# Attention and MLP mixer on one core: the first batch element's last bank sums, one scaling step and the weight conversions are placed anew

## Chip, core and metric

The kernel runs on one core of a Trainium2 chip. The metric is the device time of one execution in microseconds (us), as the median of several runs. The core has five engines with an instruction queue each: TensorE (PE in the profile; its weight loads are listed as PEld), VectorE (DVE), ScalarE (ACT), GpSimd (POOL) and SyncE (SP), which here only issues DMAs.

## What is computed

For each of 8 batch elements: attention of 12 heads with normalized q and k (448 positions, 64 dimensions a head), then an MLP mixer on the 448 x 768 result.

```python
def rmsnorm(x, g):
    return x / np.sqrt(np.mean(x * x, axis=-1, keepdims=True) + 1e-06) * g
q_n, k_n = rmsnorm(q, g_q), rmsnorm(k, g_k)
scores = (1 / np.sqrt(64)) * np.matmul(q_n, k_n.transpose(0, 1, 3, 2))
attn = softmax(scores)                      # over the last axis
attn_out = np.matmul(attn, v)               # (8, 12, 448, 64)
x = attn_out.transpose(0, 2, 1, 3).reshape(8, 448, 768)
h = np.maximum(x.transpose(0, 2, 1) @ w_tok1, 0.0) @ w_tok2     # 256 wide inside
u = x + h.transpose(0, 2, 1)
out = u + np.maximum(u @ w_ch1, 0.0) @ w_ch2                    # 1536 wide inside
```

q, k, v and the two g are float32. The four weight matrices of the mixer come in as float64; [...] the kernel reads them as pairs of 32-bit words and puts float32 numbers together from them.

## The kernel before

**Order of the work.** The heads are handled in 48 pairs, six pairs to a batch element. While the mixer of element b runs, the attention of element b+1 is worked in between, so that TensorE always has something to do. The order on TensorE, VectorE, ScalarE and GpSimd is the order in which the program issues the instructions; it is fixed by lists of items, each a cost and a function, which `merge` interleaves in proportion to their costs. Only the order on SyncE's queue is left to the scheduler.

**Attention.** `att_step(g)` is one of four steps s = 0 to 3 for two pairs of heads (t counts these groups, n is the first of the two pairs that come next). A step has scores on TensorE (L381), exponentials on ScalarE (L385), the products with v (L454), and sums of exponentials on VectorE (L422). Beside these it prepares the next two pairs: squares (L1269, L1272, ScalarE), their sums over the head (L1286, VectorE), a fold (L1294, ScalarE), a first guess of the inverse root (L1303, L1308, VectorE), Newton steps (on GpSimd, L1316 to L1319, for pairs 1 to 11 and from 20 on; else on VectorE, L1327 to L1329), the scaling of q and k by it (L343, VectorE, one instruction for each pair), and the turning of q and k so that the head dimension lies on partitions. Pairs 0 to 11 are called plain: TensorE turns them (L355) and ScalarE copies them out with g (L361, L363). Later pairs are turned by VectorE (L358) and then scaled by ScalarE (L361). In `att_step` the functions listed in `behind` go to the end of a step and those in `turns` next to its scores.

**Mixer.** The token part is two products: tok1 (L755, with the Relu by ScalarE, L758) and tok2 (L763), whose result VectorE adds from PSUM into the tile uT (L768). `m_tile()` gives out the PSUM banks of the mixer; a new product has to wait until the bank that it gets was read. The channel part of elements 1 to 7 uses a Strassen-like scheme of seven products (ch1 L879, ch2 L936) with weight units that SyncE loads (L810) from a scratch tensor in DRAM. Its right-hand sides are partly sums of quarters of uT, made by `moving_sums`: T1 and T2 by VectorE (L784, L785), T3 and T4 by GpSimd (L786, L787).

**Element 0.** Its channel part uses plain products, `first_stage(n)`, 36 stages n: 0 to 17 for w_ch1, 18 to 35 for w_ch2, six terms t to an output tile, two PSUM banks at a time (L851). After the last term of a w_ch1 tile ScalarE writes the Relu out (L863). After the last term of a w_ch2 tile ScalarE copies each of the two banks into an SBUF tile r (L860), and GpSimd adds that into uT (L861). When an output tile is done, VectorE turns it (`trans_y`, L972) and SyncE sends it (L699).

**Weight conversion.** It happens during attention and mixer of element 0, in 40 chunks, one step of the chain to a slot. Slot i does, in this order: the last step of chunk i-3 (`convert_last`, L302, VectorE), the loads of chunk i+2 (L176, SyncE), the first step of chunk i (`convert_first`: L268, L269, L271, L273, VectorE), the second step of chunk i-2 (L279, ScalarE), and the store of a finished chunk into the scratch tensor (L192, SyncE). Four chunks are token weights; the other 36 feed the 36 stages. The first 14 slots (`BEFORE`) lie in the attention of element 0, six in the token part of its mixer, and the other 24, k = 0 to 23, behind the products: slot k is placed behind product `begins(k)` in `first_items`. From the converted chunks GpSimd also makes the sums of weights that the seven products need (`make`, L204 to L207), which go to the scratch tensor (L211); to make some of them, stored chunks are read back (L221, L240).

Of the kernel before, what the change touches and what calls it, by code (L numbers as in the profile page):

```python
# [13 lines left out]
ALU = mybir.AluOpType  # L14
# [12 lines left out]
def merge(*lists):  # L27

    totals = [sum(c for c, _ in l) or 1.0 for l in lists]
    done = [0.0] * len(lists)  # L30
    at = [0] * len(lists)
    res = []
    while True:
        live = [i for i in range(len(lists)) if at[i] < len(lists[i])]
        if not live:
            return res
        i = min(live, key=lambda i: (done[i] + lists[i][at[i]][0] / 2) / totals[i])
        c, fn = lists[i][at[i]]
        at[i] += 1
        done[i] += c  # L40
        res.append((c, fn))
# [3 lines left out]
def whole(ctx, tc, shifted, pre, q, k, v, g_q, g_k, moe_w_tok1, moe_w_tok2, moe_w_ch1, moe_w_ch2, out):  # L45


    nc = tc.nc
# [61 lines left out]
    st = dict(pre.st)  # L110
# [43 lines left out]
    def columns(i):  # L154
        src = chunks[i][1][0]
        return WCOLS if chunks[i][2] is None or len(src.shape) == 3 else src.shape[-1]

    def raw_tile():
        return raw_pool.tile([P, WCOLS, 2], U32, name="raw")

    def weight_load(i):
        rows, srcs, dst = chunks[i]
        wide = srcs[0].dtype == I64
        t = raw_tile()
        flat = t[0:rows].rearrange("p n w -> p (n w)")
        if not wide:
            t = t[:].rearrange("p n w -> p (n w)").bitcast(F32)
            flat = t[0:rows]
        n = columns(i) // len(srcs) * (1 + wide)
        for k, src in enumerate(srcs):  # L170
            to = flat[:, k * n:(k + 1) * n]
            if wide:
                src = src.bitcast(U32)
            if len(src.shape) == 3:
                to = to.rearrange("p (i n) -> p i n", i=src.shape[1])
            nc.sync.dma_start(out=to, in_=src)  # L176
        st["raw", i] = t
# [12 lines left out]
    def store(j):  # L190

        nc.sync.dma_start(out=slots(j, 0, 4), in_=st["stage", j])  # L192
# [63 lines left out]
    def wide(i):  # L256
        return 0 <= i < len(chunks) and chunks[i][1][0].dtype == I64

    def words(i):

        return [st["raw", i][0:chunks[i][0], 0:columns(i), w] for w in range(2)]

    def convert_first(i):

        if wide(i):
            lo, hi = words(i)
            m = cv_sb[0:chunks[i][0], i % 2, 0:columns(i)].bitcast(U32)
            nc.vector.tensor_scalar(m, hi, 0x000FFFFF, 0x00100000, ALU.bitwise_and, ALU.bitwise_or)  # L268
            nc.vector.scalar_tensor_tensor(  # L269
                out=lo.bitcast(F32), in0=lo, scalar=2.0**-32, in1=m, op0=ALU.mult, op1=ALU.add)  # L270
            nc.vector.scalar_tensor_tensor(  # L271
                out=lo, in0=hi, scalar=0x80000000, in1=lo, op0=ALU.bitwise_and, op1=ALU.bitwise_or)
            nc.vector.tensor_scalar(hi, hi, 0x7FF00000, None, ALU.bitwise_and)  # L273

    def convert_second(i):

        if wide(i):
            e = words(i)[1]
            nc.scalar.activation(out=e, in_=e, func=AF.Relu, bias=expo_c[0:chunks[i][0], 0:1], scale=8.0)  # L279
# [14 lines left out]
    def convert_last(i):  # L294
        rows, srcs, dst = chunks[i]
        n = columns(i)
        if dst is None:
            dst = stage_home(i - len(first))
            st["stage", i - len(first)] = dst.rearrange("p (q n) -> p q n", q=4)
        if wide(i):  # L300
            lo, hi = (w.bitcast(F32) for w in words(i))
            nc.vector.scalar_tensor_tensor(  # L302
                out=dst, in0=lo, scalar=2.0**-20, in1=hi, op0=ALU.mult, op1=ALU.mult)
        else:
            nc.gpsimd.tensor_copy(out=dst, in_=st["raw", i][0:rows, 0:n])
        st.pop(("raw", i))

    def weight_items(lo, hi):

        def one(i):  # L310
            if 0 <= i - 3 < len(chunks):
                convert_last(i - 3)
            if 3 <= i and i + 2 < len(chunks):
                weight_load(i + 2)
            convert_first(i)
            convert_second(i - 2)
            if 0 <= i - 4 - len(first):
                store(i - 4 - len(first))
        return [(1.0, lambda i=i: one(i)) for i in range(lo, hi)]

# [16 lines left out]
    def scale(p):  # L339

        x, d = pre.by_rows(p, st["qk", p])
        r = st.pop(("rs", p))
        nc.vector.tensor_tensor(out=x, in0=x, in1=r.unsqueeze(2).to_broadcast(list(x.shape)), op=ALU.mult)  # L343
# [235 lines left out]
    def att_step(g):  # L579


        t, s = divmod(g, 4)
# [3 lines left out]
        items = []  # L586
# [46 lines left out]
        n = p + 2  # L633
        ahead, behind, turns = [], [], []
        f = lambda fn, *pairs: [lambda i=i: fn(i, st) for i in pairs]
        scales = lambda n: [lambda i=i: scale(i) for i in (n, n + 1)]
        if g in (1, 5):
            ahead, behind = f(pre.square, g // 4 * 2 + 4), f(pre.reduce, g // 4 * 2 + 4)
        elif g in (2, 6):
            ahead, behind = f(pre.square, g // 4 * 2 + 5), f(pre.reduce, g // 4 * 2 + 5)  # L640
        elif g in (3, 7):
            behind = pre.roots(g // 4 * 2 + 4, st)
        elif g in (4, 8):
            behind = scales(g // 4 * 2 + 2)
        if live and n < NP:
            late = n < 2 * NPAIR + 2
            if t >= NPAIR // 2 and late:
                if s == 1:
                    ahead, behind = f(pre.square, n), f(pre.reduce, n) + f(pre.square, n + 1)
                elif s == 2:  # L650
                    behind = f(pre.reduce, n + 1) + pre.roots(n, st) + scales(n)
            elif t >= NPAIR // 2:
                a, b = f(pre.square, n) + f(pre.reduce, n), f(pre.square, n + 1) + f(pre.reduce, n + 1)
                behind = (a, b + pre.roots(n, st), scales(n), [])[s]
            now = {2: [] if pre.plain(n) else [n], 3: [n, n + 1] if pre.plain(n) else [n + 1]}.get(s, [])
            turns = [lambda q=q, i=i: turn_qk(q, i) for q in now for i in (1, 0)]
# [165 lines left out]
    def r_tile(i):  # L822
        return r_pool.tile([P, 2 * HS], F32, name=f"r{i}")
# [16 lines left out]
    def first_stage(n):  # L840

        w, _, m, t = stages[n]
        wide = w is moe_w_ch2
        last = (KF if wide else KC) - 1
        if t == 0:
            st["m", 0], st["m", 1] = m_tile(), m_tile()
        a, u = st.pop(("stage", n)), st["uT", 0]
        for o in range(2):
            ps = st["m", o][:, 0:S]
            for half in range(2):  # L850
                nc.tensor.matmul(  # L851
                    out=ps, lhsT=a[:, o + 2 * half, :],
                    rhs=natural(half)[:, :, t, :] if wide else u[:, half * KC + t, :],
                    start=(t == 0 and half == 0), stop=(t == last and half == 1))
            if t < last:
                continue
            if wide:

                to, c = u[:, o * KC + m, :], r_tile(1 + o)[:]
                nc.scalar.copy(out=c, in_=ps)  # L860
                nc.gpsimd.tensor_tensor(out=to, in0=to, in1=c, op=ALU.add)  # L861
            else:
                nc.scalar.activation(  # L863
                    out=natural(o)[:, :, m, :], in_=ps.rearrange("p (i n) -> p i n", i=2), func=AF.Relu)
        st["used"].add(("stage", n))
# [150 lines left out]
    def first_items(tok, prods, some):  # L1016


        convert = weight_items(BEFORE, len(chunks) + 4)
        items = merge(tok, convert[:6])  # L1020
        for j, it in enumerate(prods[:-6]):
            items.append(it)
            items += [(0.0, convert[6 + k][1]) for k in range(len(convert) - 6) if begins(k) == j]
            if j % 2 and j < 2 * len(some):
                items.append(some[j // 2])
            if j in (26, 28):

                items += turns(0, [y_order(0)[j // 2 - 13]])
        return items, prods[-6:]

    def begins(k):


        return 2 + -(-k * 14 // 10) if k < 10 else min(k + 9, 29)

    def last_items(b):

# [6 lines left out]
    stages = stage_list()  # L1044
# [20 lines left out]
    for p in (4, 5):  # L1065
# [7 lines left out]
        out=g_t[:, 0:1], in0=g_t[:, 0:1], scalar=float(D) ** 0.5, in1=g_t[:, 1:2],  # L1073
# [27 lines left out]
    for b in range(B):  # L1101
# [4 lines left out]
        else:  # L1106
# [5 lines left out]
            begin, early = merge(tok1_items(b, 1) + early[:3 * KC], left[2:]), early[3 * KC:]  # L1112
            if b == 1 and not shifted:
                run(merge(begin, sums[5:9]))
                early, double = merge(early, sums[9:20]), merge(double, sums[20:])
                begin = []
            elif b == 1:
                early, double = merge(begin + early, sums[5:20]), merge(double, sums[20:])
                begin = []
            early = begin + early + double  # L1120
            early, last = early[:-4], early[-4:]
        lo = (b + AHEAD) * per + 1
# [281 lines left out]
```

## Time and profile before

| what | value |
|---|---|
| runs, us | 1308.59, 1310.11, 1312.26; median 1310.11 |
| the profiled execution: own time | 1311.39 us |
| its span, first to last instruction | 1309.6 us |
| granted TensorE clock, mean | 0.994 |
| idle of PE before element 0's first turns (L355), at the start | 15.2 us |
| idle of DVE in 195 to 199 us | 3.73 of 4.00 us |
| idle of DVE in 205 to 225 us | 0.72 of 20.00 us |
| idle of DVE in 256 to 275 us | 16.01 of 19.00 us |
| idle of PE in 420 to 1300 us | 1.12 of 880.00 us |

The span is what the timeline covers; the execution's own time is 1.8 us longer. The profile's times are counted from the first instruction. "idle before <- releaser" in a group's row is the time for which the engine stood still just before these instructions, and what ended it. Busy times by engine don't add up to the span, as the engines work side by side. Lines of the timeline give the start, the duration, the engine, the line of the program, the operation and the tiles; x3 at the end means that three equal instructions were put together, and the duration is then from the first start to the last end.

### The profile page before, as it was taken

What the parts mean: (1) busy time and instruction counts of PE and PEld (TensorE: products, weight loads), DVE (VectorE), ACT (ScalarE), POOL (GpSimd) and SP (SyncE); (2) the same over time, 40 slices, a digit from 0 to 9 for tenths busy, and PEclk for the clock granted to TensorE, in tenths of its full rate; (3) what the DMA queues carried; (4) which work ended last, traced back from release to release, by engine and by line L of the source; (5) the groups of instructions that cost most, each with busy time, mean ns of one, the idle gap of its engine ahead of it and who ended that gap; (6) DMA issues with size and microseconds to landing.
All of it is one profiled execution on the core that took longest, in us unless ns stands there. A gap on an engine that the chain in (4) does not pass through costs nothing.

```text
span 1309.6 us, 20269 instructions
## 1 busy us (share of the span) xinstructions
PE 1264.2 (97%) x7408; PEld 930.7 (71%) x7408; DVE 763.4 (58%) x1205; ACT 373.5 (29%) x740; POOL 350.6 (27%) x575
## 2 busy tenths in 40 slices
PE   5998999989998999999999999999999999999996
PEld 3444444447777688796778777796788868797996
DVE  6998768827774466645765366654666266433212
ACT  5652423213331133302441044302332033200100
POOL 1302410447352122221332122321242123111220
PEclk9999999999999999999999999999999999999999
DMA  9667485899979676686649667694757864385554
GB/s 207 171 190 179 122 218 149 196 257 254 246 203 225 146 186 157 156 224 121 163 122 233 141 152 175 157 235 98 169 151 174 204 139 142 117 224 132 172 177 83
DMA packets 502450, 228.07 MB, mean 174 GB/s; under 512 B 374532, under 2 KB 464004, under 8 KB 502340
## 3 DMA queue, kind: packets, MB, share of 16 engines
q1 hardware_dynamic: 489218, 224.83, 68.9%
q10 hardware_dynamic: 12994, 1.84, 0.8%
q8 instruction: 61, 1.00, 0.3%
q14 instruction: 49, 0.40, 0.1%
q0 software_dynamic: 128, 0.00, 0.0%
HBM read 187.07 MB, written 39.52 MB: 173 GB/s over the span
## 4 chain that ended last, share of the span: by engine, by line
PE 79%; DVE 9%; DMA 4%; SPq 3%; issue 2%; ACT 1%; POOL 1%; DVEq 0%; ACTq 0%; POOLq 0%
PE m_ps L936 25%; PE m_ps L879 25%; PE s_ps L381 8%; PE o_ps L454 8%; PE m_ps L763 5%; PE m_ps L755 5%; PE m_ps L851 3%; DVE raw L269 1%; DVE raw L271 1%; PE d_ps L434 1%; DMA qk_t<-in_k_dram 1%; DMA raw<-in_moe_w_ch_dram 1%; DVE stage L302 1%; DVE ms L1286 1%; DMA hb<-in_q_dram 1%
## 5 line engine op out<-in xcount | busy, mean ns | idle before, releaser
L936 PE MATMUL m_ps<-hb,unit 128*128 128x224 f32 x1764 | 339.8, 353 | 4.1 <-DVE uT L945 2.4
L936 PEld LDWEIGHTS m_ps<-hb,unit 128*128 128x128 f32 x1764 | 332.2, 190 | 15.2 <-issue 12.5
L879 PE MATMUL m_ps<-tu,unit 128*128 128x224 f32 x1008 | 201.9, 355 | 0.1
L879 PEld LDWEIGHTS m_ps<-tu,unit 128*128 128x128 f32 x1008 | 189.0, 190 | 14.6 <-issue 9.9
L385 ACT ACTIVATE e<-s_ps 128x448 f32<-128x448 f32 x294 | 138.3, 551 | 205.6 <-PE s_ps L381 197.5
L879 PE MATMUL m_ps<-uT,unit 128*128 128x224 f32 x756 | 151.1, 354 | 0.0
L879 PEld LDWEIGHTS m_ps<-uT,unit 128*128 128x128 f32 x756 | 142.2, 190 | 7.0 <-issue 4.6
L381 PE MATMUL s_ps<-qkT 64*64 64x448 f32 x1260 | 142.2, 545 | 0.4 <-ACT x L735 0.4
L454 PE MATMUL o_ps<-e,v 64*64 64x448 f32 x1148 | 129.1, 538 | 0.2
L422 DVE TENSOR_TENSOR es<-es,e 128x896 f32<-128x896 f32 x90 | 109.7, 1219 | 14.1 <-ACT e L385 8.9
L945 POOL TENSOR_TENSOR uT<-uT,r 128x448 f32<-128x448 f32 (+1 forms) x56 | 56.6, 1020 | 228.3 <-DVE r L945 140.9
L884 DVE TENSOR_TENSOR r<-m_ps,r 128x448 f32<-128x448 f32 x63 | 39.2, 622 | 108.1 <-PE m_ps L879 55.7
L945 DVE TENSOR_TENSOR uT<-uT,m_ps 128x448 f32<-128x448 f32 (+1 forms) x70 | 33.8, 499 | 110.9 <-PE m_ps L936 110.9
L381 PEld LDWEIGHTS s_ps<-qkT 64*64 64x64 f32 x1260 | 44.8, 132 | 67.1 <-issue 59.2
L454 PEld LDWEIGHTS o_ps<-e,v 64*64 64x64 f32 x1148 | 45.2, 133 | 62.4 <-issue 58.0
L884 POOL TENSOR_TENSOR hb<-r,r 128x448 f32<-128x448 f32 x21 | 24.0, 1145 | 235.6 <-ACT r L900 235.6
L763 PE MATMUL m_ps<-w_sb,h 128*128 128x448 f32 x192 | 78.3, 561 | 8.9 <-DVE uT L768 8.9
L755 PE MATMUL m_ps<-x,w_sb 112*128 112x384 f32 x256 | 84.5, 487 | 1.0 <-ACT x L735 1.0
L755 PEld LDWEIGHTS m_ps<-x,w_sb 112*128 112x128 f32 x256 | 48.4, 190 | 34.3 <-ACT x L735 1.3
L763 PEld LDWEIGHTS m_ps<-w_sb,h 128*128 128x128 f32 x192 | 36.5, 195 | 46.8 <-issue 27.8
L885 ACT ACTIVATE hb<-hb 128x448 f32<-128x448 f32 x63 | 36.3, 577 | 116.7 <-DVE hb L884 98.1
L1286 DVE TENSOR_REDUCE ms<-sq 128x28 f32<-128x896 f32 (+2 forms) x44 | 47.5, 1079 | 35.2 <-ACT sq L1272 32.2
(122 smaller groups left out, 1372.8 us busy)
## 6 DMA issues: line engine op xcount, KB each, us to landing
unit<-ws SPq DMA_DIRECT2D x294, 384.0 KB, 4.1
raw<-in_moe_w_ch_dram SPq DMA_DIRECT2D x72, 256.0 KB, 3.6
v<-in_v_dram SPq DMA_DIRECT2D x96, 112.0 KB, 3.7
xs<-xt SPq DMA_DIRECT2D x56, 168.0 KB, 4.7
x<-xs SPq DMA_DIRECT2D x14, 672.0 KB, 6.9
out_dram<-turned SPq DMA_DIRECT2D x168, 56.0 KB, 2.0
qk_t<-in_q_dram SPq DMA_DIRECT2D x144, 56.0 KB, 3.3
qk_t<-in_k_dram SPq DMA_DIRECT2D x144, 56.0 KB, 3.9
```

Of the source, the lines that this page charges most:

```text
L381: nc.tensor.matmul(out=pss[i][rows_of(i, a), 0:S], lhsT=qkT[h, 1, k * D:(k + 1) * D], rhs=qkT[h, 0, :], start=True, stop=True)
L385: nc.scalar.activation(out=e[:, i, :], in_=pss[i][:, 0:S], func=AF.Exp)
L422: nc.vector.tensor_tensor(out=es[:], in0=(es if k > 1 else st["e", t, 0])[:], in1=st["e", t, k][:], op=ALU.add)
L454: nc.tensor.matmul(out=st["o", p][a * D:(a + 1) * D, 0:S], lhsT=vt[rows, k * D:(k + 1) * D], rhs=e[rows, :], **kw)
L755: nc.tensor.matmul(out=ps[:, 0:HC], lhsT=w1_sb[0:R, c, jc * P:(jc + 1) * P], rhs=st["x", b, h][0:R, :, c, :], start=(c == 0), stop=(c == N ...
L763: nc.tensor.matmul(out=ps[:, 0:S], lhsT=st["h1", jc][:, cc * P:(cc + 1) * P], rhs=w2_sb[:, jc].rearrange("p c r -> p (c r)"), start=(jc == ...
L851: nc.tensor.matmul(out=ps, lhsT=a[:, o + 2 * half, :], rhs=natural(half)[:, :, t, :] if wide else u[:, half * KC + t, :], start=(t == 0 an ...
L879: nc.tensor.matmul(out=ps[:, j * HS:(j + 1) * HS], lhsT=w[:, t, j, :], rhs=m, start=(t == 0), stop=(t == KC - 1))
L884: add = lambda e, o, x, y: e.tensor_tensor(out=o, in0=x, in1=y, op=ALU.add)
L936: nc.tensor.matmul(out=ps[:, j * HS:(j + 1) * HS], lhsT=st["w"](j, t), rhs=hb[:, HB[what], t, :], start=(t == 0), stop=(t == KF - 1))
L945: add = lambda e, o, x, y: e.tensor_tensor(out=o, in0=x, in1=y, op=ALU.add)
L1286: self.nc.vector.tensor_reduce(out=st["ms", p][:, p % 2, lo:hi], in_=sq[:, lo:hi], axis=AX_X, op=ALU.add)
```

## The change

There are four parts.

1. Slots of the conversion are three items instead of one. `convert_first` is split into `mantissa` (L268, L269) and the rest (L271, L273). The items are: the last step with the loads; `mantissa`; the rest, the second step and the store. Each has a cost of 0.3 instead of 1.0 for the whole. `first_items` is adapted to the threefold list.
2. In `att_step` the scaling (`scales(n)`) of two plain pairs from t = 3 on moves from the end of step s = 2 to the end of step s = 3. This concerns pairs 8, 9 and pairs 10, 11.
3. In the last stage, n = 35, VectorE adds both banks from PSUM into uT, in place of ScalarE's copy and GpSimd's add.
4. `begins(k)`: from k = 10 on, slots are placed two products earlier.

```diff
-    def convert_first(i):
+    def mantissa(i):
         if wide(i):
             lo, hi = words(i)
...
             nc.vector.scalar_tensor_tensor(
                 out=lo.bitcast(F32), in0=lo, scalar=2.0**-32, in1=m, op0=ALU.mult, op1=ALU.add)
+
+    def convert_first(i):
+
+        if wide(i):
+            lo, hi = words(i)
             nc.vector.scalar_tensor_tensor(
                 out=lo, in0=hi, scalar=0x80000000, in1=lo, op0=ALU.bitwise_and, op1=ALU.bitwise_or)
             nc.vector.tensor_scalar(hi, hi, 0x7FF00000, None, ALU.bitwise_and)
...
     def weight_items(lo, hi):

-        def one(i):
+        def end(i):
             if 0 <= i - 3 < len(chunks):
                 convert_last(i - 3)
             if 3 <= i and i + 2 < len(chunks):
                 weight_load(i + 2)
+
+        def begin(i):
             convert_first(i)
             convert_second(i - 2)
             if 0 <= i - 4 - len(first):
                 store(i - 4 - len(first))
-        return [(1.0, lambda i=i: one(i)) for i in range(lo, hi)]
+        parts = (end, lambda i: mantissa(i), begin)
+        return [(0.3, lambda i=i, fn=fn: fn(i)) for i in range(lo, hi) for fn in parts]
...
                 elif s == 2:
-                    behind = f(pre.reduce, n + 1) + pre.roots(n, st) + scales(n)
+                    behind = f(pre.reduce, n + 1) + pre.roots(n, st) + scales(n) * (not pre.plain(n))
+                elif s == 3 and pre.plain(n):
+                    behind = scales(n)
...
             if wide:
                 to, c = u[:, o * KC + m, :], r_tile(1 + o)[:]
+                if n == len(stages) - 1:
+                    nc.vector.tensor_tensor(out=to, in0=to, in1=ps, op=ALU.add)
+                    continue
                 nc.scalar.copy(out=c, in_=ps)
                 nc.gpsimd.tensor_tensor(out=to, in0=to, in1=c, op=ALU.add)
...
-        items = merge(tok, convert[:6])
+        items = merge(tok, convert[:18])
         for j, it in enumerate(prods[:-6]):
             items.append(it)
-            items += [(0.0, convert[6 + k][1]) for k in range(len(convert) - 6) if begins(k) == j]
+            items += [(0.0, fn) for k in range(len(convert) // 3 - 6) if begins(k) == j
+                      for _, fn in convert[18 + 3 * k:21 + 3 * k]]
...
-        return 2 + -(-k * 14 // 10) if k < 10 else min(k + 9, 29)
+        return 2 + -(-k * 14 // 10) if k < 10 else min(k + 7, 29)
```

## The prediction

> **What bounds the kernel now.** I read the busy times first, then TensorE's waits, then the timeline round each wait, then busy times by stretch.
>
> ```profile
> PE 1264.2 (97%) x7408; PEld 930.7 (71%) x7408; DVE 763.4 (58%) x1205; ACT 373.5 (29%) x740; POOL 350.6 (27%) x575
> ```
>
> TensorE is the bound: 1264.2 of 1309.6 us. The change removes no matmul, so all it can win lies in the 45 us in which TensorE stands still, plus matmuls that run at half clock after a stop. Its waits:
>
> ```profile
> PE t_ps L355 <- DVE g_t L1072: 15.2, 1, 15.2
> PE m_ps L763 <- DVE uT L768: 8.9, 3, 4.8
> PE m_ps L851 <- ACT r L860: 2.8, 1, 2.8
> PE m_ps L936 <- DVE uT L945: 2.4, 1, 2.4
> PE m_ps L851 <- DVE stage L302: 1.5, 1, 1.5
> ```
>
> The 15.2 is the start, untouched. The change reaches row 2 (three stops: 1.56, 2.62, 4.75), row 3 and row 5: 13.2 us. The first two stops of row 2:
>
> ```profile
> 105.07 2.30 DVE L343 TENSOR_TENSOR qk_t<-qk_t,rs 112x1024 f32<-112x1024 f32 x1 [3.89 <-POOL rs L1319]
> 107.29 0.61 DVE L768 TENSOR_TENSOR uT<-uT,m_ps 128x448 f32<-128x448 f32 x1
> 107.82 1.21 DVE L343 TENSOR_TENSOR qk_t<-qk_t,rs 112x1024 f32<-112x1024 f32 x1
> 107.95 1.77 PE L763 MATMUL m_ps<-w_sb,h 128*128 128x448 f32 x4 [1.56 <-DVE uT L768]
> 112.73 3.16 PE L763 MATMUL m_ps<-w_sb,h 128*128 128x448 f32 x4 [2.62 <-DVE uT L768]
> ```
>
> VectorE waits for GpSimd's square roots, scales (L343), and the add that frees the tok2 bank (L768) stands behind. The third stop of row 2, the largest:
>
> ```profile
> 280.42 2.21 POOL L861 TENSOR_TENSOR uT<-uT,r 128x448 f32<-128x448 f32 x2
> 281.57 0.65 DVE L972 STREAM_TRANSPOSE turned<-uT 128x448 f32<-128x448 f32 x1 [22.58 <-POOL uT L861]
> 283.23 1.11 DVE L768 TENSOR_TENSOR uT<-uT,m_ps 128x448 f32<-128x448 f32 x2
> 283.87 7.84 PE L763 MATMUL m_ps<-w_sb,h 128*128 128x448 f32 x16 [4.75 <-DVE uT L768]
> ```
>
> GpSimd adds element 0's last two banks only after sums (L204 to L207) that wait for DMAs; VectorE sits 22.58 us idle at the transpose L972 that needs them; L768 is behind it, and TensorE, with both tok2 banks full, behind L768. The stop at L860:
>
> ```profile
> 199.41 2.29 DVE L422 TENSOR_TENSOR es<-es,e 128x896 f32<-128x896 f32 x2 [4.14 <-ACT e L385]
> ...
> 220.85 0.67 ACT L361 ACTIVATE qkT<-qkT,g_t 128x448 f32<-128x448 f32 x1 [2.43 <-DVE qkT L358]
> 222.07 0.94 ACT L860 COPY r<-m_ps 128x448 f32<-128x448 f32 x2
> ```
>
> ScalarE's bank copy L860 is queued behind L361, which waits for VectorE. And how full VectorE is:
>
> ```profile
> 25.00:75.00 50.00, 49.44 (x477) 23.64 (x472) 48.21 (x84) 34.46 (x68) 10.84 (x24) 1.00 0.66 179
> 205.00:225.00 20.00, 17.23 (x66) 7.72 (x65) 19.28 (x38) 6.60 (x13) 2.34 (x2) 0.93 0.63 147
> ```
>
> (Columns: stretch, length, then busy PE, PEld, DVE, ACT, POOL, clock, DMA share, GB/s.) It is 96% busy in both; from 420 us on TensorE has practically no stop, so nothing later can be won.
>
> **What the Trainium skill says.** "PSUM — Partial Sum Buffer", The four PSUM rules: GpSimd can't touch PSUM; hence a ScalarE copy ahead of L861, and VectorE needs none. "Engine vs sequencer instructions" calls the compute queues strictly FIFO; the trace agrees: L768 behind L972, L860 behind L361. "TensorE: Matmul & The Clock Gate", The HAM clock gate: idleness of about a 3.4 us window drops TensorE to half rate. The trace agrees in effect: after the stops of 2.62 and 4.75 us, matmuls start 0.75 us apart instead of 0.375; after 1.50 and 1.56 they don't. A stop over 2.5 us thus costs more than its length.
>
> **The change, part by part.**
>
> *Last banks by VectorE.* Gone: 2 copies L860 (0.53 each) on ScalarE and 2 adds L861 (1.1 each) on GpSimd, neither engine the bound. Added: 2 VectorE adds out of PSUM. L768 is this operation in this shape: 605/611/621 ns, so 1.2 us, in the 22.58 us in which VectorE is idle: free. Stage 35 ends at 265.9; adds done by 267.2, transposes (2 x 0.65) by 268.5, all before tok2 begins at 275.95. So L768 follows each tok2 product. Six tok2 sums of 4 matmuls x 0.375 = 1.5 us take 9.0 us and would end at 285.0; they end at 291.64: 6.6 us, of which 4.75 is the stop and 1.8 the half clock. What is late next: the moving sums on GpSimd (L786/L787) sit behind L204 sums that wait for loads which SyncE issues behind 8.56 us of L699 stores. The last pair ends at 306.4 where TensorE needs it at 307.6; but 1.5 us of that is only contention (1.51 each against 0.66 elsewhere), so the slack is about 2.7. The stores L699 also start earlier, as their transposes do, which clears SyncE's queue sooner. If nothing on GpSimd moves, 6.6 − 2.7 = 3.9 comes back. I take 1.1 back: **−5.5** (ends −2.7 and −6.6).
>
> *Scaling a step later, pairs 8 and 9.* The first L343s leave the place ahead of L768, so the stops 1.56 and 2.62 go, and about 2.3 us of half clock with them: −6.5 at most. But the six transposes L355 need scaled data. In the changed order VectorE does before the first L343: two L302 (1.4), three L768 (1.9), a conversion and the first parts of another (2.2 + 2.3), two L422 (2.2), about 10 us from the 104 at which it is free: 114.3. TensorE reaches L355 at about 109.4. So the stop moves from L763 to L355: 4.9 long, with about 1.2 of half clock. −6.5 + 6.1 = **−0.4** (ends −5.8 if TensorE gets there later than I count, +1.5). No DMA is issued by this step. Pairs 10 and 11 (150 to 160 us): TensorE doesn't wait there, VectorE is less full: 0 (to +1.5).
>
> *Conversions in three parts.* The same instructions (0.42 + 0.69 + 0.69 + 0.43 on VectorE, 0.68 for L302), but between them other items fit, so an add or a group sum waits at most for a third. The price: L302 needs ScalarE's L279 of the slot before, which now is issued a third of a slot ahead of it instead of a whole. The trace has two such waits, 1.9 us in all. TensorE hardly stops from 20 to 100 us (77.97 of 80 busy), so there is little to win: **−0.6** (ends −1.5, +3). SyncE's loads L176 move with the first third, ahead of the slot's other work, by at most a third of a slot: nothing.
>
> *Lead of two products more.* The slots k >= 10 start two products (3 us) earlier. Two slots (2 x 2.9 us) leave the full stretch 222 to 255 and enter the 4.14 us hole at 195 to 199. The stop of 1.50 at L302 (256.5) goes: **−1.5** (0 to −2). But 5.8 is more than 4.14, and the second slot's L302 waits for L279, behind ScalarE's L863 and squares. So the chain reduce, root, L343, L358, L361, L860 starts 1.9 later, and the stop at L860 grows: **+1.9** (ends −1, if thirds let L358 in earlier, and +4). SyncE's weight loads and stores come earlier too, into a queue full from 152 to 197; the loads run five slots ahead, which hides it.
>
> Sum: −0.4 − 0.6 − 1.5 + 1.9 − 5.5 = −6.1. Rest of the span, paced by TensorE: 0 ± 2. The profiled execution took 1311.4 (span 1309.6), 1.3 above the median of the runs: 1305.3 for it, and 1304.0 against the median 1310.1.
>
> **The rivals.**
> - *Everything clears.* −5.8 at L355, −6.6 in tok2, −1.5, and the L860 stop −1: −15, half of it likely lost to SyncE's pace: 1297. For it: VectorE in thirds. Against: the 96%.
> - *The gain in tok2 is given back downstream.* Moving sums and weight loads are tied to DMAs, not to tok2: 3.9 back, and +4 at L860: −2.7 − 0.4 − 0.6 − 1.5 + 4 = −1.2, 1309. For it: GpSimd's 9.17 us wait for a DMA just ahead of those sums. Against: the stores are issued earlier.
> - *Slower: VectorE waits for ScalarE at each L302.* 20 slots lie before 123 us; if each L302 waits 1 us (between the two waits seen, 1.43 and 0.49) for an L279 queued behind exponentials of 0.55 us, that is 20 us; VectorE's idle time from 20 to 100 (80 − 73.4 = 6.6) takes up that much, and the gains 6.1: +7.3, 1317. It decides from 0.64 us a slot. For it: VectorE at 96%. Against: ScalarE is busy only 34.46 of the 50 us of the row from 25 to 75.
> - *The scaling step does nothing but swap its wait.* That is in my forecast.
>
> **How the numbers follow.** Forecast 0.46 (1301 to 1307), everything clears 0.13 (1295 to 1301), given back 0.24 (1306 to 1312), slower 0.17 (1314 up). A measurement of this kernel tells about 0.3% (3.9 us) from no change: under 1306.2 is faster, over 1314.0 slower. The forecast's upper end falls into "same", some of the third below 1306.2; these cancel: faster 0.59, same 0.24, slower 0.17. The range 1299 to 1312 leaves out the slower case and the low end of the second.
>
> **What would show it.** Right: the wait of L763 for L768 gone; VectorE's 22.58 us wait at L972 down to nothing; tok2 of element 1 in 9 us; a new wait of L355 for L343 of about 5 us near 110; the L860 wait at 3 to 5 us; no L302 wait. Wrong: L302 waits for L279 of 0.6 us and more in many slots; a wait of L879 for L787 of over 2 us; TensorE losing time after 420 us.

## The result and the profile after

| kernel | median, us | range, us | ratio to before, 95% interval |
|---|---|---|---|
| before | 1310.03 | 1308.59 to 1312.26 | |
| changed | 1324.19 | 1322.05 to 1324.80 | 1.0105 [1.0092, 1.0118] |

The change makes the kernel 1.05% slower, some 14 us; the forecast was 6 us faster. The profiled execution of the changed kernel took 1324.19 us, its span is 1322.4 (before 1309.6: 12.8 more), with a mean granted clock of 0.986 (before 0.994). Ratios here and below are worked out from the fast runs and need not equal the quotient of the two medians beside them; one run of all was slow, 2705.76 us, one of 20 of the changed kernel in the part on SyncE's queue.

The changed kernel has other line numbers. Those used below, new = old: L307 = L302, L284 = L279, L351 = L343, L363 = L355, L773 = L763, L778 = L768, L861 = L851, L872 = L860, L430 = L422, L389 = L381, L393 = L385, L462 = L454, L891 = L879, L948 = L936, L957 = L945, L369 = L361, L1285 = L1272, L1329 to L1332 = L1316 to L1319, L796 = L786, L339 = L331 (loads of v), L1262 and L1266 = L1249 and L1253 (loads of q and k). L870 is the new add. The kernels of the experiments have numbers of their own, a few lines off.

First the busy times of the changed kernel, then its TensorE waits (total, times, longest):

```profile
PE 1269.8 (96%) x7408; PEld 934.4 (71%) x7408; DVE 761.5 (58%) x1207; ACT 373.0 (28%) x738; POOL 352.3 (27%) x573
```

```profile
PE t_ps L363 <- DVE g_t L1085: 15.1, 1, 15.1
PE m_ps L861 <- ACT r L872: 8.4, 1, 8.4
PE t_ps L363 <- issue: 6.0, 1, 6.0
PE m_ps L891 <- POOL tu L796: 3.0, 2, 2.4
PE m_ps L948 <- DVE uT L957: 3.0, 1, 3.0
PE o_ps L462 <- DMA v<-in_v_dram: 1.8, 1, 1.8
PE m_ps L765 <- ACT x L745: 1.7, 1, 1.7
```

The three stops of tok2 (8.9 us) are gone, as forecast, and so is that for L302. In their place stand a stop at the transposes (6.0), a bank copy that is 8.4 late in place of 2.8, a wait for v and one for the moving sums on GpSimd. Standing still is not all of it: the same 7408 matmuls are busy for 1269.8 us in place of 1264.2, which is 5.6 of the 12.8. The granted clock was 0.50 from 112 to 119, 194 to 197.5, 228 to 238.5, 317 to 320 and 426 to 429.5 us, 27 us in all; before, in three stretches of 3.4 us.

Where the time goes is seen from the starts of the same matmul in both traces:

| matmul (start before, us) | later by | of it in this stretch | the prediction had |
|---|---|---|---|
| first tok2 of element 0 (100.06) | 0.06 | | |
| late w_ch1 product (182.93) | 1.66 | 1.6 | −0.4 −0.6 |
| last w_ch1 product (194.18) | 6.70 | 5.0 | 0 |
| product after the bank copy (222.63) | 12.00 | 5.3 | +1.9 |
| first tok2 of element 1 (275.95) | 10.43 | −1.6 | −1.5 |
| last tok2 of element 1 (290.04) | 3.86 | −6.6 | −6.6 |
| last channel-1 product of element 1 (367.62) | 11.92 | 8.1 | +1.1 |
| last channel-2 product of all (1298.81) | 12.42 | 0.5 | 0 |

Two terms of the sum came out as worked out (−1.5, −6.6). The loss sits in the others. At the transposes, VectorE, GpSimd and TensorE in the timeline of the changed kernel:

```profile
107.37 0.65 POOL L1332 TENSOR_TENSOR rs<-nt,rs 112x32 f32<-112x32 f32 x1
...
108.73 2.74 DVE L430 TENSOR_TENSOR es<-es,e 128x896 f32<-128x896 f32 x2
111.39 0.68 DVE L268 TENSOR_SCALAR cv_sb<-raw 128x512 uint32<-128x512 uint32 x1
...
114.31 2.34 DVE L351 TENSOR_TENSOR qk_t<-qk_t,rs 112x1024 f32<-112x1024 f32 x2
...
115.62 2.47 PE L363 MATMUL t_ps<-ident,qk_t 112*128 112x112 f32 x12 [5.96 <-issue]
```

GpSimd has the roots ready at 108.0; the scaling starts at 114.31, because an addition of tok2, two sums and a conversion lie ahead of it on VectorE.

In the stretch from 182 to 223 us, SyncE and those who need its loads (changed kernel, then the kernel before):

```profile
188.75 1.33 SPq L339 DMA_DIRECT2D v<-in_v_dram  x2
...
191.98 1.53 PE L462 MATMUL o_ps<-e,v 64*64 64x448 f32 x4 [1.82 <-DMA v<-in_v_dram]
...
198.18 0.95 ACT L1285 ACTIVATE sq<-qk_t 128x896 f32<-128x896 f32 x1 [12.20 <-DMA qk_t<-in_k_dram]
...
232.84 0.67 ACT L369 ACTIVATE qkT<-qkT,g_t 128x448 f32<-128x448 f32 x1 [2.44 <-DVE qkT L366]
...
234.07 0.94 ACT L872 COPY r<-m_ps 128x448 f32<-128x448 f32 x2
```

```profile
177.33 1.30 SPq L331 DMA_DIRECT2D v<-in_v_dram  x2
```

The loads of v for pair 12 are issued 11.4 us later, and those of q and k are as late. TensorE waits for v; ScalarE stands 12.20 us before the squares, and squares, root, scaling, turning, L369 and the bank copy L872 follow in line, the copy 12.0 us later than before. SyncE's own waits from 140 to 200 us say what it stood behind, changed kernel first:

```profile
SPq L211 <- POOL few L207: 25.0, 6, 8.3
SPq L176 <- DVE cv_sb L268: 16.8, 3, 8.9
```

```profile
SPq L211 <- POOL few L207: 14.9, 6, 5.4
```

L211 sends GpSimd's weight sums; in these profiles SyncE's queue stands at it until GpSimd is done, and the loads behind it stand too. In both, v is issued about 4 us after the last of the six sends.

After tok2, the changed kernel:

```profile
286.38 9.19 PE L773 MATMUL m_ps<-w_sb,h 128*128 128x448 f32 x24
...
307.80 0.46 POOL L204 TENSOR_TENSOR raw<-raw 128x128 f32<-128x128 f32 x1 [11.21 <-DMA raw<-ws]
...
315.71 5.73 PE L891 MATMUL m_ps<-tu,unit 128*128 128x224 f32 x20 [2.36 <-POOL tu L796]
```

tok2 takes 9.2 us without a stop. Then GpSimd waits 11.21 us for a load that SyncE issues behind stores (it waited 9.17 there before, when TensorE came later), the moving sums L796 lie behind it, and TensorE waits for them.

### The profile page after: what moved, and what is told of

Read it like the earlier page. It is cut to its first block, busy times and chain, and to the rows that moved or that the text cites. A ratio compares the mean times of both kernels' runs of the same rounds, so it can differ in the third digit from the quotient of the medians.

```text
span 1322.4 us, 20257 instructions
## 1 busy us (share of the span) xinstructions
PE 1269.8 (96%) x7408; PEld 934.4 (71%) x7408; DVE 761.5 (58%) x1207; ACT 373.0 (28%) x738; POOL 352.3 (27%) x573
## 4 chain that ended last, share of the span: by engine, by line
PE 85%; DVE 6%; DMA 3%; SPq 2%; issue 2%; POOL 1%; ACT 1%; DVEq 0%; POOLq 0%; ACTq 0%
PE m_ps L948 25%; PE m_ps L891 25%; PE s_ps L389 9%; PE o_ps L462 8%; PE m_ps L765 6%; PE m_ps L773 6%; PE m_ps L861 4%; PE d_ps L442 1%; DMA raw<-in_moe_w_ch_dram 1%; DVE raw L269 1%; DMA unit<-ws 1%; DMA hb<-in_q_dram 1%; DVE raw L276 1%; PE m_ps L442 1%; SPq L1262 1%
## 5 line engine op out<-in xcount | busy, mean ns | idle before, releaser
L948 PE MATMUL m_ps<-hb,unit 128*128 128x224 f32 x1764 | 341.4, 355 | 3.0 <-DVE uT L957 3.0
L948 PEld LDWEIGHTS m_ps<-hb,unit 128*128 128x128 f32 x1764 | 333.5, 191 | 14.4 <-issue 10.8
L891 PE MATMUL m_ps<-tu,unit 128*128 128x224 f32 x1008 | 204.1, 357 | 3.1 <-POOL tu L796 3.0
L891 PEld LDWEIGHTS m_ps<-tu,unit 128*128 128x128 f32 x1008 | 190.2, 191 | 18.6 <-issue 9.2
L393 ACT ACTIVATE e<-s_ps 128x448 f32<-128x448 f32 x294 | 138.2, 550 | 200.2 <-PE s_ps L389 192.1
L891 PE MATMUL m_ps<-uT,unit 128*128 128x224 f32 x756 | 151.2, 354 | 1.1 <-DVE hb L896 1.1
L891 PEld LDWEIGHTS m_ps<-uT,unit 128*128 128x128 f32 x756 | 142.2, 190 | 8.2 <-issue 3.9
L389 PE MATMUL s_ps<-qkT 64*64 64x448 f32 x1260 | 142.2, 545 | 0.0
L462 PE MATMUL o_ps<-e,v 64*64 64x448 f32 x1148 | 132.1, 538 | 2.0 <-DMA v<-in_v_dram 1.8
L957 POOL TENSOR_TENSOR uT<-uT,r 128x448 f32<-128x448 f32 (+1 forms) x56 | 56.6, 1022 | 227.9 <-DVE r L957 141.4
L430 DVE TENSOR_TENSOR es<-es,e 128x896 f32<-128x896 f32 x90 | 109.5, 1217 | 11.7 <-ACT e L393 6.3
L957 DVE TENSOR_TENSOR uT<-uT,m_ps 128x448 f32<-128x448 f32 (+1 forms) x70 | 33.8, 499 | 112.8 <-PE m_ps L948 112.8
L462 PEld LDWEIGHTS o_ps<-e,v 64*64 64x64 f32 x1148 | 45.9, 133 | 65.9 <-issue 59.2
L389 PEld LDWEIGHTS s_ps<-qkT 64*64 64x64 f32 x1260 | 44.7, 132 | 66.7 <-issue 57.3
L773 PE MATMUL m_ps<-w_sb,h 128*128 128x448 f32 x192 | 75.3, 546 | 0.0
L778 DVE TENSOR_TENSOR uT<-uT,m_ps 128x448 f32<-128x448 f32 x48 | 29.5, 614 | 71.0 <-PE m_ps L773 70.9
```

The lines of the kernel that those rows point to most:

```text
L389: nc.tensor.matmul(out=pss[i][rows_of(i, a), 0:S], lhsT=qkT[h, 1, k * D:(k + 1) * D], rhs=qkT[h, 0, :], start=True, stop=True)
L393: nc.scalar.activation(out=e[:, i, :], in_=pss[i][:, 0:S], func=AF.Exp)
L430: nc.vector.tensor_tensor(out=es[:], in0=(es if k > 1 else st["e", t, 0])[:], in1=st["e", t, k][:], op=ALU.add)
L462: nc.tensor.matmul(out=st["o", p][a * D:(a + 1) * D, 0:S], lhsT=vt[rows, k * D:(k + 1) * D], rhs=e[rows, :], **kw)
L773: nc.tensor.matmul(out=ps[:, 0:S], lhsT=st["h1", jc][:, cc * P:(cc + 1) * P], rhs=w2_sb[:, jc].rearrange("p c r -> p (c r)"), start=(jc == ...
L891: nc.tensor.matmul(out=ps[:, j * HS:(j + 1) * HS], lhsT=w[:, t, j, :], rhs=m, start=(t == 0), stop=(t == KC - 1))
```

## Experiments: the four parts, each alone

Runs of one kernel spread by 1.5 to 10 us, often more than these effects, so kernels are compared by their ratios over several runs (4 to 20); a profile shows one execution, not always a typical one (with the thirds alone it is the fastest of six), and is used for where a wait is, not for its size to the microsecond.

**Bank sums alone**: the `if n == len(stages) - 1` part of the diff.

> Only the last bank sums by VectorE. Theory (the scaling step is the cause of the loss, the other parts are small): tok2 of element 1 takes 9 us in place of 15.7, and of these 6.6 us 3 to 6 stay: 1304 to 1307. Rival (the gain is given back downstream whatever else is done, since moving sums and weight units are tied to DMAs): 1309 to 1311, with a new wait of TensorE for the moving sums on GpSimd.

Measured 1.0008 [0.9999, 1.0017], 1311.70 us against 1311.72. TensorE's waits:

```profile
PE m_ps L763 <- DVE uT L768: 4.0, 2, 2.4
PE m_ps L882 <- POOL tu L786: 3.5, 2, 2.4
```

tok2 is 6.6 us shorter, the third of its stops is gone, and TensorE waits for T3 and T4 instead: the rival. All 6.6 are given back by 420 us.

**Scaling a step later, alone**: the `elif s == 3` part.

> Only the scaling of pairs 8 to 11 a step later. Theory: VectorE no longer stands idle while GpSimd does its Newton steps, these take longer, GpSimd's sums of weights come later, and with them SyncE's sends and all loads behind these: 5 to 12 us slower, 1315 to 1322, with the v and q/k loads of the next element several us later. Rival (the lead of the conversions is the cause): within 2 us of before.

Measured 1.0042 [1.0029, 1.0056]: 5.5 us slower (0.42% of 1311.7), with the stop at the transposes at 7.47 us. The v loads come at 180.6, only 3.3 us later than in the profile of before.

**Lead alone**: `min(k + 9, 29)` to `min(k + 7, 29)`.

> Only the conversions from the tenth on two products earlier. Theory: 0 to 2 us slower, from the wait for ScalarE's bank copy near 220 us. Rival (the lead is the cause): 5 to 12 us slower, with the wait for the bank copy at 8 us as in the changed kernel.

Measured 0.9985 [0.9975, 0.9994]: 2 us faster, against theory and rival. The wait for the bank copy is 4.7 us in place of 2.8, the +1.9 of the prediction; but the tok2 stop of 4.75 us shrinks to 0.77 as well. GpSimd's weight sums, which need the conversions that now come earlier, are done earlier, and it gets to its adds L861 at 275.8 in place of 280.4. So the lead by itself removes most of the stop that the prediction booked under the bank sums.

**Thirds alone**: `mantissa`, the three items of 0.3, and the threefold list.

> Only the conversions as three items. Theory: within 2 us of before. Rival (the slower case of the prediction: VectorE waits for ScalarE at each last step): 6 to 12 us slower, with many waits of VectorE for L279 between 20 and 123 us.

Measured 1.0041 [1.0025, 1.0056]: 5.4 us slower, but not for the rival's reason: VectorE waits for L284 once, 1.5 us. The v loads come at 181.9.

The four effects sum to +0.76%; together they give +1.05%.

## Experiments: parts in pairs and threes

> Bank sums by VectorE together with the lead of two products. Theory (both win the same wait of tok2, which the lead alone has already brought to 0.8 us): no better than the lead alone, 1308 to 1310. Rival (they add up as the prediction's sum has it): 4 us and more below the lead alone, under 1306.

Measured 0.9995 [0.9985, 1.0005]. The two win the same wait and don't add up. Whether the bank sums take back some of what the lead wins is not shown, as the intervals overlap.

> The changed kernel with the scaling left where it was. Theory (the four effects alone sum to 0.76% and the remaining 0.3% come of the scaling meeting the thirds on VectorE and GpSimd): v loads of the next pair issued at 177 to 180 us in place of 188, no wait for v, 1313 to 1316. Rival (the extra comes of the thirds with the lead): 1318 and more, v loads still late.

No scaling step: 1.0044 [1.0027, 1.0060]; v loads at 183.0, later than the theory had, but no wait for v. The time lies at the edge of the rival's (1318 and more), and TensorE waits for the bank copy about as long as in the changed kernel:

```profile
PE m_ps L859 <- ACT r L870: 8.2, 1, 8.2
```

So that wait comes of lead and thirds, which at least add up there (4.7 and 4.8 alone, 2.8 before), and not of the scaling step.

> The changed kernel with the conversions as whole slots. Theory (as for the run without the scaling step; the extra needs both): 1313 to 1316, v loads at 178 to 181 us. Rival (the extra comes of the scaling with the lead): 1318 and more.

No thirds: 1.0034 [1.0025, 1.0044]; v loads at 181.9, no wait for v. Without either of the two, 58 and 68% of the loss are gone: about the theory's 1313 to 1316 in the second case (1316.10 us beside 1312.08), above it in the first (1318.01).

> The late scaling and the thirds together, nothing else. Theory (these two meet on VectorE and GpSimd and delay SyncE's loads more than their sum): more than 0.42% + 0.41% slower, 1324 to 1328, with the v loads of the next pair at 185 us and later. Rival (additive): 1321 to 1323, v loads at 181 to 184.

Measured 1.0100 [1.0083, 1.0116]; v loads at 189.6, and TensorE waits 2.9 us for v. The two parts alone make the whole loss. Their single effects sum to 0.83%, the lower end of the interval, so that the excess is likely but not settled by the times. The profiles show a possible reason for a part of it. GpSimd's Newton steps for pairs 10 and 11, from their first start to the sum L204 behind them, take 5.2 us with the late scaling alone (145.86 to 150.99), 5.2 with all but the thirds, and 8.1 with both (149.09 to 157.19; 8.1 in the changed kernel too, 148.72 to 156.83). In the changed kernel VectorE works beside them all the time, on a second conversion and two sums (148.56 to 156.76); with the late scaling alone it stands idle from 148.7 to 154.6. Two of these GpSimd instructions, in the changed kernel:

```profile
154.70 0.94 POOL L1331 TENSOR_SCALAR nt<-nt 112x32 f32<-112x32 f32 x1
155.73 1.15 POOL L1332 TENSOR_TENSOR rs<-nt,rs 112x32 f32<-112x32 f32 x1
```

Beside an idle VectorE they take 0.22 and 0.25 us. The Trainium skill ("SBUF — State Buffer", Summary: rules for kernel authors) says that where a VectorE instruction has two inputs in SBUF and GpSimd reads SBUF, the second one to issue is blocked until the first finishes. The trace agrees in effect: each of the twelve ends 0.07 to 0.12 us after an instruction of VectorE does. That ports are the reason is not shown by a run, and the 2.9 us are less than the 7.7 by which v is issued later than with the thirds alone.

## Experiments: the cause of each part

**Where the scaling stands on VectorE.** The two scalings go right behind the scores of step s = 3, ahead of its sums:

```diff
         items.append((2.4 if s == 1 else 3.2, tiled))
+        if live and n < NP and t >= NPAIR // 2 and s == 3 and pre.plain(n):
+            items += part(scales(n))
```

> The scaling moved to the middle of the next step: right behind its scores, ahead of its sums of exponentials and of the next conversion. Theory (the new stop at the transposes comes of the place in VectorE's queue, behind 8 us of sums and conversions): no stop of over 1 us at the transposes and none at tok2 near 110, the first product of element 0's channel part 3 to 5 us earlier than before (from the start of tok2), the whole within 0.3% of before or faster, 1306 to 1312. Rival (GpSimd's roots come late when VectorE works beside them): the stop stays at 4 us or more, 1315 to 1318 as with the late scaling.

Measured 1.0015 [1.0003, 1.0027] in place of 1.0042. VectorE, then TensorE, in its timeline:

```profile
108.13 2.35 DVE L343 TENSOR_TENSOR qk_t<-qk_t,rs 112x1024 f32<-112x1024 f32 x2
```

```profile
109.45 0.58 PE L355 MATMUL t_ps<-ident,qk_t 112*128 112x112 f32 x4 [1.89 <-issue]
```

The roots are ready at 105.9. The scaling starts at 108.13, behind one addition of tok2, where with the late scaling alone it started at 112.75, and the stop falls from 7.47 to 1.89 (the theory had 1 at most): its place in VectorE's queue made the most of it. The first product of element 0 then comes 4.1 us earlier than before, counted from the start of tok2 (the theory had 3 to 5). At 130 us TensorE waits 1.46 us for v, and 3.4 of the 4.1 are gone by 135: SyncE issues that v at 128.4, no earlier than before (127.7).

**Which of the thirds.** In two kernels only the 14 slots in the attention of element 0, or only the six in its token part, were in thirds; the whole slots had a cost of 0.9.

> Only the 14 slots in the attention of element 0 as thirds, the six in the token part whole. Theory (the loss of the thirds comes of ScalarE: its second conversion step falls ahead of the copies that tok1 waits for near 80 us, after which TensorE runs at half clock): most of the 5 us, 1314 to 1317, with the wait for the copy at 1.6 us and the half clock after it. Rival (it comes of the six slots beside tok1 and tok2): within 2 us of before.

> Only the six slots in the token part as thirds. Theory: within 2 us of before. Rival: 1314 to 1317, with stores and GpSimd's first sums later and the v loads near 181 us.

Measured 1.0044 [1.0028, 1.0061] and 1.0022 [1.0013, 1.0030]. Each half costs something (v loads at 183.9 and 180.5), so neither the place in the attention nor that in the token part explains it; no half clock follows the copy near 80 us in the first of the two. What the two have in common with the thirds alone is TensorE's order, the same in all three and not that of before. Three items of 0.3 count 0.9 where a slot counted 1.0, so the list that holds element 0's mixer is shorter in costs, and `merge` puts the attention of element 1 against other products. The scores of pair 10, in the kernel before and with the thirds alone:

```profile
129.67 1.73 PE L381 MATMUL s_ps<-qkT 64*64 64x448 f32 x16
```

```profile
133.55 1.73 PE L389 MATMUL s_ps<-qkT 64*64 64x448 f32 x16
```

The run is 0.9 us late at this point; the other 3.0 are the new order. The guess of the root follows (147.67 in place of 143.80), the Newton steps, GpSimd's sums, SyncE's sends. So another kernel had the thirds with a cost of 1.0 a slot:

```diff
-        return [(0.3, lambda i=i, fn=fn: fn(i)) for i in range(lo, hi) for fn in parts]
+        return [(1.0 / 3, lambda i=i, fn=fn: fn(i)) for i in range(lo, hi) for fn in parts]
```

> The conversions as three items of a third of 1.0 each, in place of 0.3 each; nothing else of the change. Theory (the loss comes of the smaller cost, by which the next element's attention falls a product later on TensorE): within 0.15% of before, the v loads of pair 12 at 176 to 179 us. Rival (the loss comes of the three parts themselves, which stand between sums and adds on VectorE and put ScalarE's second step earlier): 0.3 to 0.5% slower, 1314 to 1317 where before is at 1310, v loads at 181 us or later.

Measured 1.0009 [0.9999, 1.0019], in place of 1.0041; v loads at 178.3, and TensorE's order at these scores is that of before again. Most of the loss was the cost written beside the items; what the three parts add is within the noise. The whole change with the cost kept was not run.

**What gives the tok2 gain back.** T3 and T4 of element 1 on VectorE, with the bank sums:

```diff
-        nc.gpsimd.tensor_tensor(out=T3, in0=B12, in1=B22, op=ALU.subtract)
-        nc.gpsimd.tensor_tensor(out=T4, in0=B21, in1=T2, op=ALU.subtract)
+        eng = nc.vector if b == 1 else nc.gpsimd
+        eng.tensor_tensor(out=T3, in0=B12, in1=B22, op=ALU.subtract)
+        eng.tensor_tensor(out=T4, in0=B21, in1=T2, op=ALU.subtract)
```

> The last bank sums by VectorE, and T3 and T4 of element 1 by VectorE too, so that they don't stand on GpSimd behind weight sums that wait for SyncE's loads. Theory (the 6.6 us won in tok2 are given back only because TensorE then waits for T3 and T4): no wait for a moving sum, 4 to 6 us faster than the bank sums alone, 1304 to 1307. Rival (it is given back to units, stores and attention in any case): within 2 us of the bank sums alone, with the same time lost elsewhere by 420 us.

Measured 1.0007 [1.0000, 1.0015]: the rival. No wait for a moving sum is left, and TensorE waits elsewhere:

```profile
PE o_ps L454 <- DVE es L422: 4.2, 1, 4.2
```

It is at 323.6 us, in the attention of element 2, whose v was issued at 318.1 and whose k landed when ScalarE had waited 5.6 us for it. Taking one wait away uncovers the next, here one behind squares that waited for a load of SyncE's.

**SyncE's queue.** The reads and sends of the first eight weight sums are issued by GpSimd, so that SyncE doesn't stand behind GpSimd's sums:

```diff
-            nc.sync.dma_start(out=slots(i, 4, 8), in_=eight(st.pop(("sum", i)))[:, 4:8])
+            (nc.gpsimd if i < FEW else nc.sync).dma_start(out=slots(i, 4, 8), in_=eight(st.pop(("sum", i)))[:, 4:8])
...
-                nc.sync.dma_start(out=eight(t)[:, 0:4], in_=slots(i, 0, 4))
+                nc.gpsimd.dma_start(out=eight(t)[:, 0:4], in_=slots(i, 0, 4))
```

On the changed kernel:

> The changed kernel with the reads and sends of the first eight weight sums issued by GpSimd in place of SyncE. Theory (SyncE stands behind GpSimd's sums, and the loads of v, q and k stand behind these on SyncE): the v loads of pair 12 at 180 us or earlier, no wait for v near 192, the wait for the bank copy near 230 down from 8.4 to 5 us or less, 6 to 10 us faster than the changed kernel, 1314 to 1318. Rival (the conversions on VectorE set the pace, and SyncE only follows them): within 3 us of the changed kernel, v loads still at 185 us or later.

On the kernel before:

> The kernel before with the same reads and sends issued by GpSimd. Theory: there the loads were early enough, so within 3 us of before in either direction. Rival (GpSimd's own issuing costs more than SyncE's wait): 4 us and more slower.

On the lead alone:

> The lead of two products with the same reads and sends issued by GpSimd. Theory: SyncE is free for the loads that pace the stretch from 170 to 240 us, so the wait for the bank copy, 4.7 us with the lead alone, falls under 3: 1304 to 1309. Rival: as with the lead alone, 1309 to 1312, or slower by what GpSimd's issuing costs.

| kernel | median, us (before beside it) | ratio to before | v loads of pair 12, us |
|---|---|---|---|
| changed, with it | 1311.56 (1310.94) | 0.9997 [0.9987, 1.0007] | 170.6 |
| before, with it | 1307.46 (1310.94) | 0.9966 [0.9952, 0.9981] | 165.5 |
| lead, with it | 1306.27 (1310.94) | 0.9959 [0.9945, 0.9973] | 164.6 |

The changed kernel is level with before again, a gain beyond the 6 to 10 us of the theory. Its TensorE waits:

```profile
PE t_ps L363 <- issue: 5.7, 1, 5.7
PE m_ps L861 <- ACT r L872: 3.4, 1, 3.4
PE m_ps L891 <- POOL tu L796: 3.3, 2, 2.4
```

The wait for v is gone, and that for the bank copy is 3.4 in place of 8.4; the stop at the transposes is still there. The same edit wins 0.34% in the kernel before, more than the 3 us that the theory allowed for: SyncE paced this stretch there already. So the fair comparison is that of both kernels with the edit: there the change still costs 0.31% (1.0031, give or take 0.18%, worked out from the two ratios), and SyncE's queue accounts for the other 0.7 of the 1.05%. With the lead the wait for the bank copy falls to 2.6, as its theory had it; between the changed kernel and this one 0.38% remain.

The edit takes two things off SyncE, the standing at L211 and the issuing itself, and no run separates them. As an estimate, ten issues of 0.36 to 0.61 us, some 4 us, are gone between 140 us and the loads of v, which come 18.2 us earlier: the standing (25.0 us) is the larger of the two.

**With the bank sums.**

> Bank sums by VectorE, with the reads and sends of the first eight weight sums issued by GpSimd. Theory (what is given back after tok2 is set by the stores and loads of 280 to 305 us on SyncE, which this doesn't touch): no better than these reads and sends alone, 1306 to 1309 where before is at 1311, and the wait for T3 and T4 on GpSimd is there. Rival (the give-back had the same cause as the rest): 4 us and more below that, 1300 to 1303.

> Bank sums by VectorE, the lead of two products, and the same reads and sends by GpSimd. Theory: as the version without the bank sums, 0.4% faster than before, 1305 to 1308. Rival (the bank sums add to it): 0.6% and more faster, under 1304.

Measured 0.9979 [0.9972, 0.9987] and 0.9973 [0.9964, 0.9981]; the first has waits of 1.1 and 2.4 us for the moving sums. The bank sums add nothing that is clear of the noise here either. The fastest version is the lead with reads and sends by GpSimd, 0.41% faster than before and ahead of both kernels of this case; that it is ahead of the versions with bank sums lies within the intervals.

## Why the prediction was wrong

**The conversions in three parts** (forecast −0.6). The step that failed is "The same instructions ... so an add or a group sum waits at most for a third". It looked only at VectorE's order within the slots. The cost beside the items, 0.9 for 1.0, moved the next element's attention on TensorE behind another product (133.55 in place of 129.67; 0.9 of the 3.9 us that run was late anyway). The part costs +0.41% by itself, and +0.09% [−0.01, +0.19] with the cost kept. The named danger, VectorE waiting for ScalarE's L279, did not come: one wait of 1.5 us where the slower rival had 20. That case was slower, but its mechanism was not the one.

**The scaling step** (forecast −0.4, and 0 for pairs 10 and 11). For pairs 8 and 9 the mechanism was right: the stop moved from L763 to L355, VectorE came to the scaling at 114.31 (forecast 114.3), and TensorE stood before it from 109.7 (forecast 109.4). That 114.3 is so exact is in part luck: the work listed began at 102.1, not at 104, and took 12.2 us with waits of 1.4 for tok2 in it, not 10. The step that failed is the sum "4.9 long, with about 1.2 of half clock": 114.3 less 109.4 is when the scaling starts, but the transposes need its result, 1.2 us later. The stop is 5.96, the half clock behind it costs up to 1.7 (granted 0.50 from 115.6 to 119.0), and that of before cost up to 1.7 and not the 2.3 counted (granted 0.83 from 110 to 120). So the term is about −5.9 + 7.7 = +1.8; the table has +1.6, with the thirds in it. "No DMA is issued by this step" was true and misled: Newton steps, weight sums, sends and loads form a line through GpSimd and SyncE, and pairs 10 and 11, booked at 0, sit at its start. With the thirds the step costs the 5.0 us at v: TensorE waits for v near 192 us only in the two kernels that have both and send from SyncE. No run separates pairs 10 and 11 from 8 and 9. The 5.3 before the bank copy come without the scaling step too.

**SyncE.** "The loads run five slots ahead, which hides it" was said of the weight loads. The loads that decided were those of v, q and k on the same queue, and the prediction did not ask who waits behind L211 there. With GpSimd's reads and sends off it the change costs 0.31% in place of 1.05%.

**Lead** (forecast +1.9 −1.5). Right in both terms, taken alone: the copy waits 4.7 in place of 2.8, and the products from 222 to 276 gain 1.6 in the changed kernel. That the thirds make the same chain later as well, to 8.2 us with both, was not seen, nor that the lead also frees the third tok2 stop, so that most of the −5.5 was counted for a part that is not needed for it.

**Bank sums** (forecast −5.5). The 6.6 us in tok2 are exact. The give-back "I take 1.1 back" was mis-sized: 8.1 us come back between 290 and 368 in the changed kernel, all 6.6 in the part alone. The second rival, given back downstream by GpSimd's moving sums, described it; its 3.9 was too small as well, since behind T3 and T4 there stood other waits (323.6 us, with these two on VectorE).

What stays open: how much of the excess of scaling and thirds together over their sum is real (0.17%, within the intervals); which transfer ends the wait at 323.6 us; and what makes up the 0.31% that the change costs with SyncE relieved.

## What to carry to other kernels

Ask of each queue not only what is issued in it, but what waits at its head: here the sends of GpSimd's sums stood ahead of the loads, and GpSimd, 27% busy, so came to hold up TensorE; with them off that queue 0.7 of the 1.05% was gone. A cost written for a planner is part of the program: splitting an item must keep its sum, or work elsewhere moves. And before a stop's length is booked as a gain, ask what else would remove it and which transfer is due right after it: of 6.6 us won in tok2 nothing was left 100 us later.

## What the runs showed of the hardware that had not been expected

GpSimd's small root instructions (112x32) took 0.22 to 0.25 us with VectorE idle and up to 1.15 beside VectorE's conversions and sums: a chain of twelve went from 5.2 to 8.1 us. The line of 2.5 us that the prediction drew for stops of TensorE does not hold: with the thirds alone a stop of 1.65 us (81.29) was followed by a granted clock of 0.50 from 82.2 to 85.4, in the changed kernel the same stop (81.42) was not, and with the bank sums alone a stop of 2.36 (111.22) was followed by 1.00 up to 116 us. GpSimd takes 0.75 to 0.89 us to issue such a read or send, SyncE 0.36 to 0.61, and yet moving these off SyncE won 0.34%. The Trainium skill ("DMA: Bandwidth & Descriptors", Issuing engines are not separate DMA queues) says that issuing from several engines saves only the time to start a DMA, usually small beside the DMA itself. Here more was saved: the loads of v came 18.2 us earlier in the changed kernel, where the issues taken off SyncE before them are some 4 us, and the measurement decides.
